# A third up product out of seven small ones, and a down product with a shorter list of waits, in a Strassen mixture-of-experts kernel

## The chip, the cores and the metric

The kernel runs on one core of a Trainium2 chip. The core has five engines that run side by side, each with its own instruction queue: TensorE (PE, matrix products; PEld is its loading of the stationary operand), VectorE (DVE), ScalarE (ACT), GpSimd (POOL) and SyncE (SP, which here only issues transfers). The metric is the device time of one execution in microseconds: the median of the runs shown.

## The reference

Linear attention makes a matrix x of 4608 tokens by 512; a mixture of 8 experts follows, in which every expert sees every token and the routing only weights the sum.

```
P = exp(x @ w_gate - max)              # 4608 x 8, then 8 rounds of scaling rows and columns
out = 0
for e in range(8):
    h   = maximum(x @ w1[e], 0)        # up:   4608x512 @ 512x1024
    out += P[:, e:e+1] * (h @ w2[e])   # down: 4608x1024 @ 1024x512
```

Nearly all the arithmetic is in the up and down products of the eight experts.

## The kernel before

**Stages.** The first 200 us are the attention, with parts of expert 0's products laid between its steps. Then come the routing and the rest of expert 0 in plain products, then experts 1 to 7.

**Seven products for eight.** Experts 1 to 7 use a Strassen form: a 2 by 2 block product is made of seven block products instead of eight, with sums of blocks taken before and after. Tokens stand in nine groups of 512; the first eight are worked in four pairs, the ninth by itself. Within a pair the hidden features are split in two halves (`fp` 0 and 1). One pair and one half make a *unit*; an expert has eight units of pairs and one unit of the ninth group. A unit holds the seven up products of its own pair and half, and the seven down products of a group whose up work was done earlier.

**An up product, plain.** `wide` (line 1467) gives for each of two feature blocks `q` two matmuls with 512 moving columns: four matmuls of 512 for a product. Line 1471 records these.

**An up product, fine.** In experts 2 to 7 two of the seven (the weights "12" with the tokens "21", and "s1" with "t1") are themselves made of seven: `fine` (line 1588 on) gives seven matmuls of 256 columns (line 1603) in four steps a1 to a4, and the sums between them: in a1 two ACT copies of 128x256, one into the side buffer `m5` (1615) and one within PSUM (1617); in a2 a DVE addition (1624); in a3 an ACT copy (1608); and at the end one addition of `m5` (`last`, on DVE at 1644, or `later`, on POOL at 1638). The next step's matmul needs the copy before it, so between a1, a2, a3 and a4 other matmuls have to fill PE. A dictionary `INNER` names the fine products. The product "11", whose steps are called x, is plain: x10 and x11 are its two halves in the written order, and `keep` copies its banks to the buffers k1 on ACT (1666). The order names the steps of fine products wa to wd and ya to yd, with wk and yk for what follows.

**Operands.** In expert 1 the sums of token blocks are made once on DVE (`sub`, line 1239) and sent to DRAM (`Xd` and `Xp` plain, `Xi` for fine products, seven blocks instead of four). In experts 2 to 7 `load_fine` (1385) brings each pair's operands back on the SP queue (1393) into places in the space of `xT`, taken in turn: four places for fine operands (`FINE_X`), two of them used by a pair, and six for plain ones (`PLAIN_X`), five used by a pair. A load waits until the last reader of its place is done. The sums of weight blocks are taken for every expert on DVE, four short additions for each fine product (`fine_up`, 1270 on).

**Down.** `down7` multiplies quarters of h and sums of quarters `S` with blocks of w2, in seven products X1, Y1, Z1, X2, X3, Z2, X4 of eight 256-column matmuls each (1462). X1 reads only the quarter h(0,0). The results leave PSUM on DVE (1855), or on ACT (1867) with the addition on POOL (1870).

**What sets the order.** Every operation is given to a planner with an engine, an estimated duration, and the buffers and keys it reads and writes; the planner lays them on the engines in order of start, ties going to the one written earlier. The written order within a unit is a string of step names, one of 19 in `UNITS`: 0 to 8 for expert 1, 9 to 16 for the eight pair units of experts 2 to 7, 17 for the ninth group, and 18 for the ninth group of the last expert, where it goes first. Each engine then executes its instructions in the planned order. PSUM has eight banks that all products share. DVE operations on two SBUF operands are marked as sharing a port with POOL; the planner keeps the two apart, and a POOL operation planned close behind such a DVE operation is given a wait for it.

Of the kernel before, what the change touches and what calls it, by code (L numbers as in the profile page):

```python
# [349 lines left out]
def kernel(  # L350
# [137 lines left out]
        R[f"H{slot}"].make = lambda i, slot=slot: late["hs"][:, slot]  # L488
    ring("s_p", [128, 1024], BF16, "T", 4)
    ring("s_p", [128, 2, 256], FP32, "U", 4)  # L490
    ring("s_p", [128, 2, 2, 256], BF16, "X", 4)
    ring("s_p", [128, 2, 256], FP32, "K", 4)
    R["K"].make = lambda i: R["X"].make(i).rearrange("p a k c -> p (a k c)").bitcast(
# [843 lines left out]
    class Turns:  # L1337
# [4 lines left out]
        def next(self):  # L1342
# [3 lines left out]
            return p[0], p[1], first  # L1346

    pairs = [(g, g + 1) for g in range(0, 8, 2)]
    INNER = {"12": "21", "s1": "t1"}
    FINE_W = {n: space(3, 1024 * (i + 4 - len(INNER)), 1024, "nfc", (4, 2, 128)) for i, n in enumerate(INNER)}  # L1350
    FINE_X = Turns([space(i // 2, 1792 * (i % 2), 1792, "nc", (7, 256)) for i in range(4)])
    PLAIN_X = Turns([space(2 + i // 4, 1024 * (i % 4), 1024, "akc", (2, 2, 256))
                     for i in range(5 if len(INNER) > 2 else 6)])
    M5 = Turns([space(i, 3584, 512, "c", (256,), FP32) for i in range(2)])

    Xi = {(g[0], n): dram.tile([128, 7, 256], BF16, name=f"xi{g[0]}{n}")
          for g in pairs for n in INNER.values()}
    Xp = {(g[0], n): dram.tile([128, 2, 2, 256], BF16, name=f"xp{g[0]}{n}") for g in pairs
# [212 lines left out]
    def up49(A, fp, X, H, gs, r0):  # L1571
# [16 lines left out]
        def fine(bank, an, xn, more=(), takes=(), wk=(), out_c=None):  # L1588

            f, r = A[an]  # L1590
            s, rs = A[an + "*"]
            t, rt = X[xn]
            r = r + rs + rt + list(r0)
            m5, key, first = M5.next()

            def a(q, k):
                return lambda: f()[:, k, 128 * (2 * fp + q):][:, 0:128]

            def sf(n):
                return lambda: s()[:, n, fp, :]  # L1600

            def mul(q, n, lhs, rhs, more=(), takes=(), start=False, wk=()):
                pe(256, lambda: nc.tensor.matmul(  # L1603
                    halves_of(bank[q], n)(), lhsT=lhs(), rhs=t()[:, rhs, :], start=start,
                    stop=True, skip_group_check=True), r + list(more), [bank[q], *wk], takes)

            def copy(q, n, q2, n2):
                act(293, lambda: nc.scalar.copy(
                    out=halves_of(bank[q], n)(), in_=halves_of(bank[q2], n2)()),
                    [bank[q2]], [bank[q]])  # L1610

            def a1():
                mul(1, 0, sf(0), 3, more, takes, True, wk)
                mul(1, 1, a(0, 0), 0)
                act(256, lambda: nc.scalar.copy(out=m5(), in_=halves_of(bank[1], 0)()),
                    [bank[1]], [key, *first])
                act(293, lambda: nc.scalar.copy(
                    out=halves_of(bank[0], 0)(), in_=halves_of(bank[1], 1)()),
                    [bank[1]], [bank[0]])

            def a2():
                mul(1, 1, sf(1), 4)
                mul(0, 0, a(0, 1), 1)
                dve(256, lambda: nc.vector.tensor_tensor(  # L1624
                    out=halves_of(bank[0], 1)(), in0=halves_of(bank[1], 1)(), in1=m5(),
                    op=ALU.add), [bank[1], key], [bank[0]])

            def a3():
                mul(1, 1, sf(2), 5)
                mul(0, 1, sf(3), 2)  # L1630
                if out_c is None:
                    copy(1, 0, 1, 1)

            def a4():
                mul(1, 0, a(1, 1), 6, start=out_c is not None)

            def later(to, w):
                pool(330, lambda: nc.gpsimd.tensor_tensor(  # L1638
                    out=to(), in0=to(), in1=m5(), op=ALU.add), [key], [w])

            def last(out_=None, w=None, pm=False):
                if pm:
                    return later(out_, w)
                dve(256, lambda: nc.vector.tensor_tensor(
                    out=out_() if out_ else halves_of(bank[1], 1)(),
                    in0=halves_of(bank[1], 1)(), in1=m5(), op=ALU.add),
                    [bank[1], key] if out_ else [key], [w] if out_ else [bank[1]])

            return a1, a2, a3, a4, last
# [63 lines left out]
                        [y[q]])  # L1713

        def yk():
            ys[4](lambda: k1[1]()[:, 1, :], (k1[1], 1), True)
            for q in range(2):
                add(y, q, k1, 1, 1)

        def wk():  # L1720
            keep(w, 0, u)
            act(256, lambda: nc.scalar.copy(out=u[1]()[:, 0, :], in_=halves_of(w[1], 0)()),
                [w[1]], [(u[1], 0)])
            ws[4](lambda: u[1]()[:, 1, :], (u[1], 1))

        def x2(q):
            prod(x, q, "s2", "t2")
# [58 lines left out]
    def down7(e, g, H, B7):  # L1786
# [94 lines left out]
        x, y, z = new("P1"), new("PO"), new("P1")  # L1881

        def X1():
            prod(x, a(0, 0), "11", hk(0, 0), True, sk(1) + hk(1, 0),
                 [("D", e, g)])
            act(512, lambda: nc.scalar.copy(out=y(), in_=x()), [x], [y])

# [31 lines left out]

    END = "X1 p2 Y1 X2 Z1 p3 X3 Z2 X4 p0 p1".split()  # L1920
    UNITS = [o.split() for o in (
# [27 lines left out]
    turns = [int(i) for i in (  # L1949
        "0 1 2 3 4 5 6 7 8 9 10 11 12 13 14 15 16 17 9 10 11 12 13 14 15 16 17 9 10 11 12 "  # L1950
        "13 14 15 16 17 9 10 11 12 13 14 15 16 17 9 10 11 12 13 14 15 16 17 18 9 10 11 12 "
# [102 lines left out]
```

## Time and profile before

| | |
|---|---|
| median of 3 runs (lowest, highest) | 1012.7 us (1012.62, 1013.81) |
| the profiled execution | 1013.51 us, of which the span from first to last instruction is 1011.7 us |
| granted TensorE clock | 1.000 |
| PE matmuls | 8232 |
| DVE, ACT, POOL instructions | 1911, 1786, 466 |
| periods of experts 4, 5 and 6 | 108.1, 107.9 and 108.2 us, from the recurring long piece in the chain (548.95, 657.08, 764.98, 873.22) |

The busy share of an engine is the union of its instructions' spans. A matmul's span is longer than the distance to the next, since matmuls overlap: 273 ns against 109 ns for 256 columns. So the work of PE is read from the chain of work, where a piece of n matmuls in a row has its length beside it, and not from the mean of one. What one engine waited for another is a view of its own.

### The profile page before, as it was taken

Reading aid. Unit: us, or ns where it says so; the run is one execution under the profiler, and the core shown is the slowest. Engines: PE = TensorE matmul, PEld = TensorE weight load, DVE = VectorE, ACT = ScalarE, POOL = GpSimd, SP = SyncE. Lnnn points to the kernel's source line nnn. Section 1 sums busy time; section 2 is a strip of 40 time slices with the busy share of each in tenths; the row PEclk is TensorE's granted clock in tenths of the full one; section 3 lists DMA queues with packets and bytes.
Section 4 is the critical chain, followed back from the end, with each engine's and each line's share of the span. In section 5 each row is a group of like instructions: output and inputs, shape, how many; then the busy total and the mean of one; then the engine's idle time right before and its main releaser. Section 6 shows DMA issues by size and latency. Waiting matters only on the chain.

```text
span 1011.7 us, 22631 instructions
## 1 busy us (share of the span) xinstructions
PE 997.0 (99%) x8232; PEld 712.1 (70%) x8232; DVE 879.9 (87%) x1911; ACT 771.8 (76%) x1786; POOL 412.9 (41%) x466
## 2 busy tenths in 40 slices
PE   7899999999999999999999999999999999999998
PEld 4666666644666877777777777787778777787776
DVE  7999998987888988889888889889888988889885
ACT  7999999845987777767777777777776777677773
POOL 5778674400133333343333334433343343433333
PEclk9999999999999999999999999999999999999999
DMA  9999979181135522273237232452228222724553
GB/s 237 200 200 177 169 141 140 38 172 48 58 103 114 164 89 90 66 173 106 82 96 146 82 113 88 94 146 89 90 75 203 89 90 66 139 90 135 173 180 125
DMA packets 129680, 123.32 MB, mean 122 GB/s; under 512 B 55712, under 2 KB 98720, under 8 KB 129568
## 3 DMA queue, kind: packets, MB, share of 16 engines
q1 hardware_dynamic: 97616, 97.82, 34.5%
q0 software_dynamic: 31648, 23.86, 16.3%
q8 instruction: 64, 1.05, 0.4%
q14 instruction: 48, 0.39, 0.1%
q10 hardware_dynamic: 304, 0.20, 0.1%
HBM read 117.78 MB, written 18.74 MB: 135 GB/s over the span
## 4 chain that ended last, share of the span: by engine, by line
PE 94%; DMA 2%; ACT 2%; DVE 1%; issue 0%; SPq 0%; DVEq 0%
PE ps L1462 42%; PE ps L1471 25%; PE ps L621 18%; PE ps L1603 7%; PE ps L904 2%; DMA acc<-in_q_dram 1%; DMA xT<-wx 1%; ACT q L617 1%; ACT k L617 1%; DVE wx L613 0%; PE ps L751 0%; ACT wx L617 0%; PE ps L933 0%; DVE m L613 0%; DVE ps L912 0%
## 5 line engine op out<-in xcount | busy, mean ns | idle before, releaser
L1870 POOL TENSOR_TENSOR acc<-acc,hx 128x512 f32<-128x512 f32 x186 | 235.1, 1269 | 429.4 <-ACT hx L1867 125.9
L1462 PEld LDWEIGHTS <-hs 128*128 128x128 bf16 x1984 | 193.8, 98 | 54.1 <-issue 0.2
L1867 ACT ACTIVATE hx<-ps,P 128x256 f32<-128x256 f32 x372 | 157.5, 478 | 63.0 <-PE ps L1462 52.6
L1855 DVE SCALAR_TENSOR_TENSOR acc<-ps,P,acc 128x256 f32<-128x256 f32 x372 | 162.6, 478 | 46.7 <-PE ps L1462 33.8
L1471 PE MATMUL ps<-xT,T 128*128 128x512 bf16 x608 | 179.1, 379 | 0.0
L1462 PEld LDWEIGHTS <-hx 128*128 128x128 bf16 x1488 | 145.4, 98 | 32.8
L1462 PE MATMUL ps<-hx,hs 128*128 128x256 bf16 x992 | 134.8, 273 | 0.1
L1670 DVE CUSTOM_DVE_ANT_0 hs<-ps,U 128x512 bf16<-128x512 f32 x192 | 126.9, 682 | 5.7 <-PE ps L1471 5.1
L1676 ACT ACTIVATE hs<-ps 128x512 bf16<-128x512 f32 x96 | 57.5, 599 | 56.5 <-PE ps L1471 56.0
L1471 PEld LDWEIGHTS <-T 128*128 128x128 bf16 x672 | 65.6, 98 | 36.0
L1603 PE MATMUL ps<-xT 128*128 128x256 bf16 x384 | 88.0, 273 | 0.2 <-DVE ps L1624 0.2
L1471 PE MATMUL ps<-xT,wx 128*128 128x512 bf16 x288 | 84.1, 379 | 0.0
L1462 PE MATMUL ps<-wx,hs 128*128 128x256 bf16 x560 | 76.9, 273 | 0.0
L621 PE MATMUL ps<-w,hx 128*128 128x512 bf16 x288 | 73.1, 379 | 0.0
L621 PE MATMUL ps<-xT,w 128*128 128x512 bf16 x288 | 72.9, 379 | 0.0
L1638 POOL TENSOR_TENSOR X<-X,xT 128x256 f32<-128x256 f32 x48 | 34.9, 726 | 91.2 <-DVE hx L1239 34.3
L1728 ACT COPY ps<-ps 128x512 f32<-128x512 f32 x96 | 55.1, 581 | 17.0 <-DVE acc L1855 12.3
L1670 DVE CUSTOM_DVE_ANT_0 hs<-ps,X 128x512 bf16<-128x512 f32 x96 | 65.5, 682 | 2.6 <-PE ps L1603 2.3
L1462 PE MATMUL ps<-wx,hx 128*128 128x256 bf16 x496 | 67.4, 273 | 0.0
L1666 ACT COPY X<-ps 128x512 f32<-128x512 f32 x96 | 57.1, 602 | 13.4 <-PE ps L1471 13.4
L1462 PE MATMUL ps<-hx 128*128 128x256 bf16 x496 | 66.8, 273 | 0.0
L613 DVE TENSOR_REDUCE m<-ps 128x4 f32<-128x512 f32 x88 | 58.7, 679 | 3.7 <-PE ps L621 1.9
(172 smaller groups left out, 2132.0 us busy)
## 6 DMA issues: line engine op xcount, KB each, us to landing
xT<-xd SPq DMA_DIRECT2D x72, 256.0 KB, 2.8
xT<-xp SPq DMA_DIRECT2D x48, 256.0 KB, 2.9
xT<-xi SPq DMA_DIRECT2D x24, 448.0 KB, 3.7
wx<-in_moe_w_dram POOLq DMA_DIRECT2D x8, 1024.0 KB, 12.8
v_m<-in_v_dram SPq DMA_DIRECT2D x15, 512.0 KB, 5.9
out_dram<-acc SPq DMA_DIRECT2D x14, 512.0 KB, 2.9
w<-in_moe_w_dram POOLq DMA_DIRECT2D x6, 1024.0 KB, 11.5
qk<-in_k_dram POOLq DMA_DIRECT2D x12, 256.0 KB, 5.7
```

What stands on the lines that cost most here:

```text
L613: dve(el, lambda: nc.vector.tensor_reduce(out=dst(), in_=src(), axis=AX.X, op=ALU.max, apply_absolute_value=True), r, w)
L621: nc.tensor.matmul(out_, lhsT=lhsT, rhs=rhs, start=start, stop=stop)
L1462: pe(256, lambda i=i, k=k, z=z: nc.tensor.matmul(bank()[:, 256 * i:256 * i + 256], lhsT=lhs(k, i), rhs=rhs(k), start=first and z, stop=k = ...
L1471: pe(512, lambda k=k: nc.tensor.matmul(bank().rearrange("p (a b) -> p a b", a=2), lhsT=lhs(k), rhs=rhs(k), start=first and k == 0, stop=k ...
L1603: pe(256, lambda: nc.tensor.matmul(halves_of(bank[q], n)(), lhsT=lhs(), rhs=t()[:, rhs, :], start=start, stop=True, skip_group_check=True) ...
L1666: act(512, lambda: nc.scalar.copy(out=flat(to[q])(), in_=bank[q]()), [bank[q]], [(to[q], 0), (to[q], 1)])
L1670: dve(515, lambda: nc.vector._custom_dve(ADD_SAT, out=out_(q, i, j), in0=bank[q]().rearrange("p (a b) -> p a b", a=2), in1=to[q](), s0=3.0 ...
L1676: act(512, lambda: nc.scalar.activation(out=out_(q, i, j), in_=bank[q]().rearrange("p (a b) -> p a b", a=2), func=ACT.Relu, bias=0.0, scal ...
L1728: act(512, lambda: nc.scalar.copy(out=z[q](), in_=x[q]()), [x[q]], [z[q]])
L1855: dve(320, lambda n=n, ts=ts: nc.vector.scalar_tensor_tensor(out=acc[g][:, ts, 256 * j:256 * j + 256], in0=bank()[:, 256 * n:256 * n + 256 ...
L1867: act(370, lambda n=n: nc.scalar.activation(out=u()[:, n, :], in_=bank()[:, 256 * n:256 * n + 256], func=ACT.Copy, bias=0.0, scale=P[:, 4 ...
L1870: pool(695, lambda: nc.gpsimd.tensor_tensor(out=acc[g][:, 2 * i:2 * i + 2, 256 * j:256 * j + 256], in0=acc[g][:, 2 * i:2 * i + 2, 256 * j: ...
```

## The change

The product "11" joins the fine ones, in experts 2 to 7: x10 and x11 become xa, xb, xc, xd and xk. With three fine products the fine weights take a third place, the plain token operands five places instead of six (a pair now uses four), and the four fine places now serve three operands of a pair. `m5` gets a third place, in a buffer of its own. After the product "s1" (wk) the addition of `m5` goes from DVE to POOL, and the half copy on ACT before it becomes a whole one. In experts 2 to 7 X1 no longer waits for h(1,0) and for the sum S1. All 19 written orders are new.

```
-    INNER = {"12": "21", "s1": "t1"}
+    INNER = {"11": "11", "12": "21", "s1": "t1"}
...
+    ring("s_p", [128, 256], FP32, "M", 1)
+    m5 = new("M")
+    m5.slot = 0
+    M5.places.append((m5, "M", []))
...
-            def later(to, w):
-                pool(330, lambda: nc.gpsimd.tensor_tensor(
-                    out=to(), in0=to(), in1=m5(), op=ALU.add), [key], [w])
-
-            def last(out_=None, w=None, pm=False):
+            def later(to):
+                for b in to:
+                    pool(330, lambda b=b: nc.gpsimd.tensor_tensor(
+                        out=b()[:, 1, :], in0=b()[:, 1, :], in1=m5(), op=ALU.add),
+                        [key], [(b, 1)])
+
+            def last(out_=None, w=None, pm=()):
                 if pm:
-                    return later(out_, w)
+                    return later(pm)
...
         def yk():
-            ys[4](lambda: k1[1]()[:, 1, :], (k1[1], 1), True)
+            ys[4](pm=k1[1:])
...
         def wk():
             keep(w, 0, u)
-            act(256, lambda: nc.scalar.copy(out=u[1]()[:, 0, :], in_=halves_of(w[1], 0)()),
-                [w[1]], [(u[1], 0)])
-            ws[4](lambda: u[1]()[:, 1, :], (u[1], 1))
+            keep(w, 1, u)
+            ws[4](pm=u[1:])
...
         def X1():
-            prod(x, a(0, 0), "11", hk(0, 0), True, sk(1) + hk(1, 0),
+            prod(x, a(0, 0), "11", hk(0, 0), True, [] if e > 1 else sk(1) + hk(1, 0),
                  [("D", e, g)])
```

The steps of x that the change now calls are in the kernel already, behind the test `"11" in INNER`:

```
        if "11" in INNER:
            xs = fine(x, "11", "11", [], own)
...
        def xk():
            xs[4]()
            for q in range(2):
                if "12" in INNER:
                    keep(x, q, k1)
```

The new orders of the eight pair units (9 to 16):

```
+        "xa xb wa X1 Z1 ya X2 wb xc Y1 X3 xd yb X4 wc yc xk Z2 yd wd wk x20 yk x21 x30 x40 "
+        "w21 x31 x41 w20",
+        "xa Z1 xb wa X1 wb Z2 xc xd wc ya xk x21 X2 wd yb wk yc x20 x30 Y1 x40 X3 yd x31 "
+        "w21 yk w20 X4 x41",
+        "X1 wa wb xa Z1 xb wc ya Y1 X2 wd xc yb xd xk yc Z2 wk x20 X3 yd x21 w21 w20 x30 yk "
+        "x31 X4 x40 x41",
+        "xa X1 Z1 Y1 xb wa ya wb xc X2 yb xd wc xk x20 wd wk x21 yc x31 X3 Z2 x30 x41 x40 "
+        "yd yk w20 w21 X4",
+        "wa wb X1 xa Y1 Z1 xb wc ya yb xc wd xd yc X2 X3 yd xk x21 wk X4 x20 w21 x30 yk x31 "
+        "Z2 w20 x40 x41",
+        "X1 xa xb wa ya yb yc wb wc xc xd xk yd Z1 X2 wd wk x21 Z2 x20 yk X3 X4 x31 x30 Y1 "
+        "x41 w21 x40 w20",
+        "wa xa xb xc X1 wb xd Z1 xk wc X2 Y1 x21 wd ya x20 Z2 wk X3 w21 w20 x30 x31 yb X4 "
+        "yc x41 yd x40 yk",
+        "xa X1 Z1 xb X2 xc xd xk wa Z2 ya yb yc X3 wb x20 x21 yd X4 wc wd yk wk x30 Y1 x40 "
+        "x31 w20 x41 w21",
```

38 rows, old and new, of the table UNITS are left out of this document.

## The prediction

> **What bounds the kernel now.** I read the page's busy times first, then the chain of work, then what PE waited for, then a table by stage.
>
> ```profile
> PE 997.0 (99%) x8232; PEld 712.1 (70%) x8232; DVE 879.9 (87%) x1911; ACT 771.8 (76%) x1786; POOL 412.9 (41%) x466
> PE 94%; DMA 2%; ACT 2%; DVE 1%; issue 0%; SPq 0%; DVEq 0%
> ```
>
> PE is busy 99% of the span and makes 94% of the chain. A busy PE need not be PE at its pace, so the chain is read in order of time, for the distance between matmuls:
>
> ```profile
> 657.08 13.54 PE ps L1462 x124
> 764.98 13.54 PE ps L1462 x124
> 995.08 1.73 PE ps L621 x8
> ```
>
> 124 matmuls of 256 columns in a row take 13.54 us, 109.2 ns each; eight of 512 columns take 1.73 us, 216.3 ns each. With these two prices an expert can be counted. A pair unit has five plain up products of four 512s (20 x 216.3 = 4.33 us), two fine ones of seven 256s (14 x 109.2 = 1.53 us) and a down of 56 x 109.2 = 6.12 us: 11.97 us. Eight of them, and 112 x 109.2 = 12.23 us for the ninth group, are 108.0 us. The two long pieces above lie 107.9 us apart. So in experts 2 to 7 PE has matmuls without a gap, and what PE executes is the time. What PE waited for, from 260 us to 1005 us, is one line:
>
> ```profile
> PE ps L1603 <- DVE ps L1624: 0.2, 1, 0.2
> ```
>
> How much room the others have is in the table by stage (us, then PE, PEld, DVE, ACT, POOL busy, clock, DMA share). The first four rows are experts 3 to 6, 108 us each; the fifth is the start of expert 1; the last two are attention:
>
> ```profile
> 441.00:549.00 108.00, 108.00 (x835) 81.36 (x833) 95.22 (x199) 79.08 (x187) 41.53 (x38) 1.00 0.40 107
> 549.00:657.00 108.00, 107.94 (x833) 81.14 (x831) 95.01 (x199) 78.84 (x185) 41.33 (x38) 1.00 0.40 107
> 657.00:765.00 108.00, 108.00 (x835) 81.36 (x834) 95.23 (x199) 79.01 (x186) 41.57 (x38) 1.00 0.39 107
> 765.00:873.00 108.00, 107.82 (x832) 81.10 (x831) 94.79 (x199) 78.86 (x185) 41.19 (x38) 1.00 0.39 107
> ...
> 258.00:335.00 77.00, 77.00 (x525) 51.10 (x524) 66.17 (x157) 65.29 (x133) 23.08 (x19) 1.00 0.41 107
> ...
> 20.00:60.00 40.00, 36.49 (x454) 25.65 (x454) 39.07 (x91) 39.84 (x101) 31.00 (x53) 1.00 1.26 203
> 60.00:203.00 143.00, 142.82 (x1695) 93.95 (x1692) 131.06 (x308) 135.42 (x330) 91.40 (x147) 1.00 0.89 140
> ```
>
> DVE is at 88% in the experts and ACT at 73%, and PE loses nothing by it. The attention rows show where that ends: from 60 to 203 us, with DVE at 91.7% and ACT at 94.7%, PE lacks 0.18 us of 143; from 20 to 60 us, with DVE at 97.7% and ACT at 99.6%, it lacks 3.51 of 40, 8.8%. The prices of what is added are in the groups by shape:
>
> ```profile
> L1624 DVE TENSOR_TENSOR ps<-ps,xT 128x256 f32<-128x256 f32 x96 | 40.5, 427 | 13.8 <-PE ps L1603 10.1 <-ACT ps L1886 1.4 <-PE ps L1462 1.0
> L1617 ACT COPY ps<-ps 128x256 f32<-128x256 f32 x96 | 36.9, 385 | 0.4
> L1615 ACT COPY xT<-ps 128x256 f32<-128x256 f32 x96 | 36.8, 383 | 8.7 <-PE ps L1603 8.5
> L1608 ACT COPY ps<-ps 128x256 f32<-128x256 f32 x96 | 36.6, 382 | 8.3 <-PE ps L1603 7.7
> L1638 POOL TENSOR_TENSOR X<-X,xT 128x256 f32<-128x256 f32 x48 | 34.9, 726 | 91.2 <-DVE hx L1239 34.3 <-ACT xT L1615 28.3 <-ACT U L1666 19.7
> L1644 DVE TENSOR_TENSOR U<-ps,xT 128x256 f32<-128x256 f32 x48 | 20.1, 419 | 11.9 <-PE ps L1603 11.1
> ```
>
> The counts give the number of units: 96 for two fine products, 48 units.
>
> **The change, part by part.** *The matmuls.* In each of 48 units four 512s (865.2 ns) give way to seven 256s (764.4 ns): 100.8 ns less, 4.84 us in all, and all of it on the path that sets the end, since PE is that path. PE will have 8232 + 48 x 3 = 8376 matmuls.
>
> Three more weight loads a unit come with it, 98 ns each in the groups of PEld. They go beside the matmul before: the 124 matmuls above each had a load of their own and still kept 109.2 ns. The page "TensorE: Matmul & The Clock Gate" of the Trainium skill (section "Back-to-back issue gap") puts it otherwise: in a stream of loads and matmuls it gives about 81 ns a matmul at 128 columns and about 131 at 512. An estimate half-way down its line, 97.7 ns at 256, would make seven small ones 684 ns against 524 for four large ones, a loss of 160 ns a unit or 7.7 us in all. This trace disagrees, 109.2 and 216.3 ns, and the sum goes by the trace.
>
> *DVE.* A unit gains the addition in a2 (427 ns) and the one at the end of x (same form as 1644, taken at 419), and loses the one after w (419): +0.43 us. Each expert gains four short weight sums of 280 ns (the 128x256 bf16 form of line 1239), 1.1 us. An expert goes from 95.1 to 95.1 + 8 x 0.43 + 1.1 = 99.6 us, in 107.9 - 0.8 = 107.1: 93%. *ACT* gains 383 + 385 + 382 in the three copies and 605 - 388 = 217 where half a copy becomes whole, 1.37 us a unit; an expert goes from 79.0 to 89.9 us, 84%. *POOL* gains one addition of 0.73 us a unit, 41.4 to 47.2 us, 44%. None of this is on the path as long as PE finds its banks free and its copies made. The cover is the idle time of DVE, 7.5 us in an expert, and the other matmuls between two steps of a fine product; gone, it costs PE what DVE is late.
>
> What such waits cost at 93% this trace does not show, so I bound it. At best it is nothing, as at 88% now; below nothing it can't be, because PE has no wait left to lose. At worst it is the row from 20 to 60 us, 8.8%, for those stretches in which DVE comes to 97% or more. The nearest row is 60 to 203 us, DVE at 91.7% and ACT fuller than here: 0.18/143 = 0.13%. I take it: 0.13% of 6 x 107.1 us is 0.8 us.
>
> *The addition after w, now on POOL.* Its readers are the DVE additions of x31 and w2. Queued behind it on POOL are the down additions of line 1870 (1.27 us each); these free the buffers of line 1867 on ACT, which waited for POOL only 3.5 us in five times over the whole run. POOL is idle 56% of the time, so I cost it at nothing; if POOL were late, DVE would stand in its queue before x31, and that is the second rival's place.
>
> *X1 without its waits.* PE waits for nothing there now, so nothing is gained; the freedom is in the new order. X1's bank is then taken earlier, a matter of the banks that I put to the 0.8 us. *Expert 1.* A pair's "11" goes to DRAM as seven blocks: 16 DVE sums of 280 ns (4.5 us), four more transfers on SP in all, and four times a buffer of the ring X, for about 3 us each (four sums and a landing of 2.0 us). In the row from 258 us DVE would rise from 66.2 to at most 70.7 of 77 us, 92%, and PE has no wait there: by the same 0.13% 0.1 us, within the rounding. *Loads.* A fine operand has 448 KB against 256, 192 KB more for each of 24 pairs; the DMA engines are at 40%. The load is covered as long as its place comes free in time: that is the first rival. *The new orders* take away nothing, since PE has no gap to close; what they may add is the waits bounded above.
>
> Sum: -4.84 + 0.8 = -4.0 us. The profiled execution took 1013.51 us (its span of 1011.7 and 1.8 around it) and would take 1009.5; it stands 0.8 above the median of the runs, 1012.7, which becomes 1008.7.
>
> **Rivals.** *A late fine operand takes it back.* Until now a pair's two fine operands had two places that the pair before did not use. Now three share four places: "t1" goes where "11" of the pair before lay and "21" where its "t1" was, so the loads wait for xd and wd in the unit before. Counted in the written orders at the two matmul prices, PE has 8.9, 6.7 and 8.9 us of other work between xd and the next wa at the three changes of pair within an expert, and 9.0 to 12.4 us between wd and ya. The fine operands land in 3.7 to 7.6 us (medians of the four groups); the longest landing of an operand between 441 and 873 us was 9.4, when weights stream beside it. So mostly there is time. If one load per expert took 7.6 us against 6.7, PE would lose 0.9 x 6 = 5.4 us, and the time would be 1013.3: no gain. Smaller lateness ends between that and the forecast.
>
> *DVE becomes the bound: slower.* The busiest 12 us of expert 4 shows DVE at 11.45:
>
> ```profile
> 585.00:597.00 12.00, 12.00 (x94) 8.97 (x92) 11.45 (x25) 9.15 (x22) 4.24 (x5) 1.00 0.31 101
> ```
>
> Add 0.43 us and shorten the unit to 11.87, and DVE is full. A full DVE costs PE 8.8% by the row from 20 to 60 us, 1.04 us a unit. One such unit per expert costs 6.3 us in all (1014.1), two 12.5 us (1020.4). It decides from 0.8 us an expert, where the gain is gone. Against it: the work of an expert is laid anew, and the mean of 93% leaves 7.5 us that another order can spread.
>
> The Trainium skill's page "SBUF — State Buffer" (section "SBUF: two separate sides") has a rule that speaks for this rival: a DVE operation with two SBUF inputs and a GpSimd operation hold their port for a whole instruction, and the other blocks. By that rule 48 more POOL operations of 0.73 us could hold DVE up by at most 5.8 us an expert, which would fill it to 98%. In this trace the DVE sums of 512 have a median of 417 to 426 ns with POOL at 41%, so the order keeps them apart so far.
>
> *Weight loads pace the small matmuls.* If a load no longer went beside a matmul, seven times 98 + 109 ns is 1.45 us against 0.87, +28 us in all: 1040.5. The 124 matmuls at 109.2 ns speak against it.
>
> *The step doesn't come about.* Were the planned order to leave "11" plain somewhere, the matmuls would be fewer than 8376 and the time 1012.7; the edit gives no such way.
>
> **How the numbers follow.** From 0.2%, 2.0 us, on a difference can be told. The forecast has 0.65 (1007.4 to 1010: no waits at all gives 1012.7 - 4.8 = 1007.9, and runs differ by some 0.5). The late operand has 0.14, of which 0.05 stays faster and 0.09 ends within 0.2%. DVE as the bound has 0.18, the weight loads 0.02, the step that doesn't come about 0.01. Faster 0.70, same 0.10, slower 0.20. The range goes from 1007.4 to 1014.2: it takes in the forecast, the late operand and one full unit per expert, and leaves out two full units and the weight loads, with less than 0.2.
>
> **What would show it.** Right: 8376 matmuls, 1008 of them at line 1603's place and 992 at 1471's; DVE 1911 + 48 + 16 + 24 = 1999 and ACT 1786 + 144 = 1930 instructions; the recurring long piece about 107.1 us apart; DVE at about 93% and ACT 84% in an expert; waits of PE for DVE and ACT after 260 us of about a microsecond in all. Wrong: PE waiting for a transfer into xT at the start of a pair (first rival); PE waiting for DVE additions in the fine steps, or for banks that DVE frees, with DVE near 97% (second); chain pieces with more than 110 ns a small matmul (third).

## The result, and the profile after

The changed kernel takes 1010.4 us, the median of 8 runs (1008.93 to 1012.13), against 1012.61 for the kernel before on the same chip (8 runs, 1011.9 to 1014.79): a ratio of 0.9976, with a 95% interval of 0.9965 to 0.9986, or -2.2 us. Run once more on another chip, it took 1010.15 against 1012.78. The profiled execution took 1010.62 (span 1008.8), 2.9 less than the one of before, which stood 0.9 above its own median.

Lines have moved by one to six: the down matmul is at 1466 now, the plain up matmul at 1475, the fine one at 1607, the sum of 512 at 1240, the addition of a2 at 1628, the POOL addition at 1643. The busy times of the changed kernel, from its page:

```profile
PE 991.1 (98%) x8339; PEld 726.9 (72%) x8376; DVE 899.2 (89%) x1999; ACT 810.2 (80%) x1930; POOL 446.8 (44%) x514
```

8376 weight loads, 1999 DVE and 1930 ACT instructions are the counts that were forecast: "11" is fine in all 48 units. (37 records of the 8376 matmuls are missing in this trace, all of them of 512 columns, at line 622.) The chain of work breaks off where those records are missing, so its shares say little; read in order of time (start, duration, engine, tile, line, count) it still shows the experts:

```profile
444.13 11.35 PE ps L1466 x104
551.26 11.35 PE ps L1466 x104
658.39 11.35 PE ps L1466 x104
765.52 11.35 PE ps L1466 x104
...
997.00 1.73 PE ps L622 x8
```

The piece comes back every 107.13 us, where the kernel before needed 107.9 to 108.2, and 11.35/104 is 109.1 ns a small matmul. The table by stage of the changed kernel (us, then PE, PEld, DVE, ACT, POOL busy, clock, DMA share) has experts 3 and 4 and then the start of expert 1:

```profile
441.00:548.00 107.00, 107.00 (x857) 83.65 (x856) 97.17 (x210) 85.23 (x210) 46.98 (x45) 1.00 0.41 115
548.00:655.00 107.00, 107.00 (x857) 83.71 (x856) 97.16 (x211) 85.25 (x210) 46.95 (x45) 1.00 0.40 115
...
258.00:335.00 77.00, 75.74 (x514) 50.03 (x513) 70.07 (x174) 64.66 (x132) 22.32 (x18) 1.00 0.47 126
```

DVE has gone from 88% to 90.8%, ACT from 73% to 79.7%, and PE is still busy for 107.00 of 107.00 us. The third row is new: PE lacks 1.26 us of 77, where it lacked nothing before. What PE waited for from 260 to 1005 us is again one line, now at that place:

```profile
PE ps L1475 <- DVE hs L1530: 1.3, 2, 0.7
```

So the fine experts gave what was forecast, and part of it is given back in expert 1, which has no fine product on PE at all. To see how much, I set the distance between the starts of matmuls against their pace: 109.2 ns for each one of 256 columns and 215.8 ns for each one of 512, missing records filled in from the weight loads. (The 40 matmuls of 8 and 24 columns in the routing are taken at their own distances, 25 and 28 ns.) What is over is called *lost time* below. PE's work by this count is 976.98 us before and 972.22 after, -4.76. This figure is the number of matmuls times their pace, the sum of the forecast again; that the pace was kept is what the period of 107.13 us shows. Lost time from 203 us on is 0.7 us before; it is 3.1 in the profile of the changed kernel and 2.1 in that of its second run. By stage:

| lost time, us | before | after | second run of after |
|---|---|---|---|
| 203 to 320 (expert 0's rest, expert 1) | 0.09 | 0.47 | 0.26 |
| 320 to 335 (expert 1, last pair) | 0.01 | 1.58 | 0.83 |
| 350 to 441 (turn to expert 2, and expert 2) | 0.01 | 0.26 | 0.26 |
| 441 to 873 (four experts) | 0.60 | 0.12 | 0.12 |
| 873 to the last matmul | 0.00 | 0.67 | 0.67 |

From the start of the last matmul to the end of the span it takes 4.25 us where it took 3.87; what makes the difference wasn't followed. -4.76 + 1.4 to 2.4 + 0.4 is -2.0 to -3.0, where the medians lie. The rest between the two profiles, 0.9 us, lies before 203 us, in the attention, which the change doesn't touch.

**Where the 1.3 us arise.** The transfers between 300 and 335 us, first of the kernel before, then of the changed one (size, median us from issue to landing):

```profile
w<-in_moe_w_dram POOLq DMA_DIRECT2D x2, 1024.0 KB, 11.5
...
xi6t<-X SPq DMA_DIRECT2D x1, 256.0 KB, 2.0
```

```profile
w<-in_moe_w_dram POOLq DMA_DIRECT2D x2, 1024.0 KB, 11.9
...
xi6t<-X SPq DMA_DIRECT2D x1, 256.0 KB, 8.0
```

This store of the last fine operand takes 8.0 us to land where it took 2.0. The issue of expert 2's weights on POOL, before and after, points at the cause:

```profile
319.78 1.69 POOL L516 DMA_DIRECT2D w<-in_moe_w_dram  x2
```

```profile
314.54 1.69 POOL L517 DMA_DIRECT2D w<-in_moe_w_dram  x2
```

Before, the weights were issued 1.9 us behind the store (317.93), and the store was all but alone. The new orders let them start 5.2 us earlier, 1.8 us ahead of the store (316.38), which then lands beside 2 MB of weights, at 324.4. It holds a buffer of the ring X, and DVE and then PE stand behind that (timelines of the changed kernel, DVE and PE; idle time before the instruction and its releaser in brackets):

```profile
324.41 0.42 DVE L1240 TENSOR_TENSOR X<-xT 128x512 bf16<-128x512 bf16 x1 [1.70 <-DMA xi6t<-X]
```

```profile
329.63 0.38 PE L1475 MATMUL ps<-X,wx 128*128 128x512 bf16 x1 [0.54 <-DVE hs L1530]
330.72 0.81 PE L1475 MATMUL ps<-X,wx 128*128 128x512 bf16 x3 [0.71 <-DVE hs L1530]
```

DVE stands for 1.70 us, and its evictions behind that come 0.54 and 0.71 us late for PE.

### The profile page after: what moved, and what is told of

The parts are those of the page before. It is cut to its first block, busy times and chain, and to the rows that moved or that the text cites. A ratio compares the mean times of both kernels' runs of the same rounds, so it can differ in the third digit from the quotient of the medians.

```text
span 1008.8 us, 23319 instructions
## 1 busy us (share of the span) xinstructions
PE 991.1 (98%) x8339; PEld 726.9 (72%) x8376; DVE 899.2 (89%) x1999; ACT 810.2 (80%) x1930; POOL 446.8 (44%) x514
## 4 chain that ended last, share of the span: by engine, by line
PE 66%; DVE 1%; issue 0%
PE ps L1466 39%; PE ps L1475 16%; PE ps L1607 11%; PE ps L622 1%; DVE hs L1676 0%; DVE hs L1530 0%; DVE acc L1860 0%; DVE X L1240 0%; DVE acc L1774 0%; DVE ps L1628 0%
## 5 line engine op out<-in xcount | busy, mean ns | idle before, releaser
L1475 PE MATMUL ps<-xT,T 128*128 128x512 bf16 x608 | 167.4, 379 | 0.0
L1676 DVE CUSTOM_DVE_ANT_0 hs<-ps,U 128x512 bf16<-128x512 f32 x192 | 123.7, 683 | 4.4 <-PE ps L1475 1.4
L1607 PE MATMUL ps<-xT 128*128 128x256 bf16 x576 | 127.4, 272 | 0.1
L1466 PE MATMUL ps<-wx,hx 128*128 128x256 bf16 x496 | 73.7, 273 | 0.0
L1466 PE MATMUL ps<-hx 128*128 128x256 bf16 x496 | 72.8, 273 | 0.0
L622 PE MATMUL ps<-w,hx 128*128 128x512 bf16 x274 | 69.9, 379 | 0.6
L1607 PEld LDWEIGHTS <-xT 128*128 128x128 bf16 x576 | 56.3, 98 | 16.6 <-issue 0.2
L1466 PE MATMUL ps<-w,hx 128*128 128x256 bf16 x432 | 63.0, 273 | 0.0
L1612 ACT COPY ps<-ps 128x256 f32<-128x256 f32 x144 | 53.0, 376 | 9.9 <-PE ps L1607 9.9
L1466 PE MATMUL ps<-w,hs 128*128 128x256 bf16 x432 | 60.9, 273 | 0.0
```

The source lines that it names most:

```text
L622: nc.tensor.matmul(out_, lhsT=lhsT, rhs=rhs, start=start, stop=stop)
L1466: pe(256, lambda i=i, k=k, z=z: nc.tensor.matmul(bank()[:, 256 * i:256 * i + 256], lhsT=lhs(k, i), rhs=rhs(k), start=first and z, stop=k = ...
L1475: pe(512, lambda k=k: nc.tensor.matmul(bank().rearrange("p (a b) -> p a b", a=2), lhsT=lhs(k), rhs=rhs(k), start=first and k == 0, stop=k ...
L1607: pe(256, lambda: nc.tensor.matmul(halves_of(bank[q], n)(), lhsT=lhs(), rhs=t()[:, rhs, :], start=start, stop=True, skip_group_check=True) ...
L1612: act(293, lambda: nc.scalar.copy(out=halves_of(bank[q], n)(), in_=halves_of(bank[q2], n2)()), [bank[q2]], [bank[q]])
L1676: dve(515, lambda: nc.vector._custom_dve(ADD_SAT, out=out_(q, i, j), in0=bank[q]().rearrange("p (a b) -> p a b", a=2), in1=to[q](), s0=3.0 ...
```

## The experiments

Two theories stood against each other at first. **A**: the loss is that held buffer in expert 1, and the load of DVE costs nothing. **B**: DVE, fuller by the fine "11", takes the gain back. Beside them I took the change apart: X1's waits, the fineness of "11", the POOL addition, the four places of fine operands. Each ratio is to the kernel before, run on the same chip (medians 1012.78, 1012.78 and 1012.99 in the three groups); with each comes its distance to the changed kernel, taken at 1010.15.

**The changed kernel again.**

> The changed kernel again, as the yardstick of this group. Theory A (the product saves 4.8 us of PE work; about 1.6 us of new waits are given back, 1.25 of them in expert 1 at one place): 2 to 3 us faster than before, DVE near 97.2 us of 107 in an expert, the same two waits of PE for the addition of expert 1 at 329 to 331 us. Theory B (the rest of the forecast was lost to DVE being full): the same time, but waits of PE for DVE in every expert.

Measured: 1010.15 us, ratio 0.9971 (0.996 to 0.9983). The same loss is in its profile, in the same place, but smaller: the store takes 7.3 us to land, and PE waits 0.7 us, once, for line 1530.

**Was it the fineness of "11"?** In `eleven_plain_again` "11" is plain as before, and all else of the change stays (X1 without waits, the additions on POOL, the new orders with the fine steps taken out of them). Here and below a diff is against the changed kernel where nothing else is said.

```
-    INNER = {"11": "11", "12": "21", "s1": "t1"}
+    INNER = {"12": "21", "s1": "t1"}
...
-        "xa Z1 xb wa X1 wb Z2 xc xd wc ya xk x21 X2 wd yb wk yc x20 x30 Y1 x40 X3 yd x31 "
-        "w21 yk w20 X4 x41",
+        "x10 Z1 wa X1 wb Z2 x11 wc ya x21 X2 wd yb wk yc x20 x30 Y1 x40 X3 yd x31 "
+        "w21 yk w20 X4 x41",
```

> The changed kernel with product eleven plain as before (INNER of two; in the new orders xa stands for x10, xc for x11, and xb, xd and xk fall out); X1 freed, the addition after w on POOL, the new orders stay. PE's work is that of before, 4.8 us more than the changed kernel. Theory A (the gain is the work of the product, the rest gives nothing): 1012.5 to 1014 us, at or above before. Rival (freed X1, POOL and new orders bring part of the gain): under 1012 us.

Measured: 1013.52 us, ratio 1.0009 (1.0 to 1.0018), 3.4 above the changed kernel. PE's counted work is back at 976.98. So the rest of the change gives nothing by itself (in orders made for three fine products), and the fine "11" is worth 3.1 to 3.4 us net of the waits that it brings.

**X1 freed alone, and X1 bound again.** `x1_freed_alone` is the kernel before, its old orders kept, with only X1's waits shortened (diff against the kernel before); `x1_waits_again` is the changed kernel with X1's waits as they were. These waits are entries in the planner's list: X1 reads only h(0,0), so what they change is the order in which the operations are laid.

```
-            prod(x, a(0, 0), "11", hk(0, 0), True, sk(1) + hk(1, 0),
+            prod(x, a(0, 0), "11", hk(0, 0), True, [] if e > 1 else sk(1) + hk(1, 0),
```

```
-            prod(x, a(0, 0), "11", hk(0, 0), True, [] if e > 1 else sk(1) + hk(1, 0),
+            prod(x, a(0, 0), "11", hk(0, 0), True, sk(1) + hk(1, 0),
```

> The kernel before, with nothing but X1 freed of its waits for h(1,0) and S1 in experts 2 to 7; old orders, eleven plain. As the prediction had it: nothing to gain, within 0.5 us of before. Rival (the freedom is worth something by itself): PE's few waits, 0.6 us after 260 us, can't give more than 0.6 us; a loss would come from banks taken earlier.

> The changed kernel, with X1 waiting for h(1,0) and S1 again; the written orders stay. Theory A (PE has other matmuls there): within 0.7 us of the changed kernel. Rival (the three fine products need X1 early to fill PE between their steps): waits of PE at the beginning of units, 0.1 us or more a unit, 5 us or more in all.

Measured: freed alone 1016.16 us, ratio 1.0033 (1.002 to 1.0046), slower by 3.4; bound again 1060.72 us, ratio 1.0467 (1.0453 to 1.0481), 50.6 above the changed kernel. That was the largest effect of all, and the prediction had nothing of the kind: in `x1_waits_again` PE loses 8.2 to 8.5 us in each of experts 2 to 6 and 9.7 in the last. The two longest of its waits there, from 203 us on:

```profile
PE ps L1607 <- ACT ps L1621: 10.2, 31, 0.6
PE ps L1607 <- DVE ps L1628: 8.3, 18, 0.7
```

Both are in the fine steps, behind the copies and additions between them. DVE is busy for less of its time there than in the changed kernel (91.58 of 107 us against 97.17), and ACT as well (80.92 against 85.23): the engines are not full, PE only has to sit through their chain. One such place in expert 3, PE's timeline of `x1_waits_again`:

```profile
487.24 0.27 PE L1607 MATMUL ps<-xT 128*128 128x256 bf16 x1
...
487.78 0.27 PE L1607 MATMUL ps<-xT,wx 128*128 128x256 bf16 x1
488.62 0.27 PE L1607 MATMUL ps<-xT 128*128 128x256 bf16 x1 [0.57 <-ACT ps L1621]
488.73 0.27 PE L1607 MATMUL ps<-xT,wx 128*128 128x256 bf16 x1
489.19 0.27 PE L1607 MATMUL ps<-xT 128*128 128x256 bf16 x1 [0.19 <-ACT ps L1621]
...
490.42 0.38 PE L1607 MATMUL ps<-xT 128*128 128x256 bf16 x2 [0.69 <-DVE ps L1628]
```

Six fine matmuls stand in a row, 0.65 us of work, and then each next step has to wait for a copy or an addition. A down product with its short list of waits is what fills these gaps in the changed kernel. With the old orders, which don't need it, the same freedom costs 3.4 us. PE's lost time from 203 us on is 2.7 us there against 0.7, and from 441 to 873 us waits of 1.5 us out of 1.7 end with line 1624's additions: a shorter list of waits alone moves the planned order, and not for the better.

**The addition after w back on DVE, then both.** First `w_addition_on_dve`, then `both_additions_on_dve`, which has this and `yk`'s addition on DVE as well. They put load on DVE and take it off POOL; for w, ACT's copy is halved again too.

```
-            keep(w, 1, u)
-            ws[4](pm=u[1:])
+            act(256, lambda: nc.scalar.copy(out=u[1]()[:, 0, :], in_=halves_of(w[1], 0)()),
+                [w[1]], [(u[1], 0)])
+            ws[4](lambda: u[1]()[:, 1, :], (u[1], 1))
```

```
-            ys[4](pm=k1[1:])
+            ys[4]()
```

> The changed kernel, with the addition after w on DVE again and the half copy before it. DVE gets 8 x 0.42 = 3.4 us more in an expert, ACT 1.7 and POOL 5.8 less. Theory A (DVE has room up to about 95%): within 1 us of the changed kernel. Theory B (DVE near its limit; between 0.13% of waits at 91.7% and 8.8% at 97.7% a straight line gives about 3% at 94%): some 10 to 20 us slower than the changed kernel.

> The changed kernel with the additions after w and after y both on DVE (none on POOL). Against the run with w's alone another 0.42 us a unit, 3.4 us an expert, on DVE. If PE's loss grows with DVE's load along the line from the changed kernel (97.2 of 107 us, next to no waits) over w alone (98.8 of 107, 0.6 us an expert): 1 to 1.5 us of waits an expert, 1017 to 1020 us. If the loss in the run with w alone came from the later end of its chain and not from the load: about 1014 us.

Measured: 1013.75 us, ratio 1.0008 (0.9999 to 1.0016), and 1017.51, ratio 1.0047 (1.0034 to 1.006). Moving the one addition to POOL is thus worth 3.6 us, and the second 3.8. For the first, neither theory had the size: A had nothing much, B three times that and more. Expert 3 in the table by stage, of the first and of the second kernel:

```profile
441.00:548.00 107.00, 106.96 (x852) 83.08 (x850) 98.53 (x217) 83.63 (x209) 41.36 (x37) 1.00 0.40 113
```

```profile
441.00:548.00 107.00, 106.88 (x847) 82.55 (x846) 100.56 (x223) 82.38 (x207) 35.74 (x29) 1.00 0.41 113
```

Beside the row of the changed kernel this makes a scale over experts 3 to 6: with DVE at 90.8% PE loses 0.03 us an expert, at 92.1 to 92.5% 0.55 to 0.69, at 94.0 to 94.8% 1.0 to 1.5. Operations of DVE end 1.8 of the 2.5 us that PE waits in these four experts in the first of the two kernels, and 2.7 of 4.5 in the second; ACT ends the rest. So B's mechanism is there, and the changed kernel stands just ahead of it. But the share alone doesn't set the loss: each edit also moves the planned order, and the kernel before lost 0.15 us an expert with DVE at 88%, the one with X1 freed 0.35 to 0.57.

**The weights behind the last store.** In `weights_after_last_store` both of expert 2's weight loads are planned behind the stores of the last pair's fine operands; in `w2_after_last_store` only the second is. As with X1, this binds the planner and puts no wait into the transfer itself.

```
-        w1, w2 = load_w(e, ["late", ("acc", 4, 0, 0)] if e > 1 else ["late"])
+        w1, w2 = load_w(e, (["late", ("acc", 4, 0, 0)] if e > 1 else ["late"])
+                        + [("Xi", 6, n, 2) for n in INNER.values() if e == 2])
```

```
-                r, [(w, i, j) for i in range(2) for j in range(2)])
+                r + ([("Xi", 6, n, 2) for n in INNER.values()] if e == 2 and w is w2 else []),
+                [(w, i, j) for i in range(2) for j in range(2)])
```

> The weight loads of expert 2 wait for the last stores of fine operands. Theory A (the last store of a fine operand lands 8.0 us late because the weights stream beside it; its buffer of ring X is then late for the sums of the ninth group, DVE stands 1.7 us, PE 1.25): that store lands in about 2 us, both waits go, 1.2 us less than the changed kernel unaltered, 3.4 to 4 us less than before. Rival (DVE is simply too full in expert 1 with 16 more sums): the same sums stand there, PE still waits about a microsecond, the time is that of the changed kernel.

> Only the second of expert 2's two weight loads (w2, which the down products need a unit later) waits for the last stores of fine operands; w1 goes as in the changed kernel. Theory A (the late landing is what holds DVE in expert 1, and holding back both loads only moved the loss to the beginning of expert 2, where w1 came late): the last store lands in about 5 us instead of 8, PE's waits at 329 to 331 us go, none comes at the beginning of expert 2, 0.7 to 1.3 us less than the changed kernel, so 3.3 to 3.9 us less than before. Rival (any delay of the weights costs more than it gives): slower than the changed kernel by 1 us or more.

Measured: 1015.69 us, ratio 1.0027 (1.0019 to 1.0036), 5.5 above the changed kernel, and 1011.01, ratio 0.9985 (0.9976 to 0.9994), 0.9 above it by the medians (the interval overlaps that of the changed kernel). The store of the first of these, from its transfers between 300 and 335 us, and then what PE waited for from 260 us on:

```profile
xi6t<-X SPq DMA_DIRECT2D x1, 256.0 KB, 2.0
```

```profile
PE ps L1466 <- ACT hx L1872: 2.0, 2, 1.0
PE ps L1607 <- DVE ps L1628: 1.2, 2, 1.0
```

This shows the cause named above: with the weights issued at 321.36, behind it, the store lands in 2.0 us again, and PE's waits behind line 1530 are gone. (In the other kernel, w1 went off 1.9 us ahead of the store and w2 4.2 us behind it, before it had landed; the store took 7.0 us.) But the time is not saved. PE loses 1.15 us from 334.0 to 335.2, the first of its two waits for line 1872, and 4.3 us from 350 to 441, in expert 2, at the second of them and at fine steps whose filling now lies elsewhere.

**The buffer instead of the weights.** The same wait can go another way: the four temporaries that the store holds are put into the ring T, for the last pair alone (`last_temporary_elsewhere`) or for all (`all_temporaries_elsewhere`). The core of the edit, first of the former, then of the latter:

```
-        y = new("X")
+        last = g == 6
+        y = new("T" if last else "X")
```

```
-        y = new("X")
+        y = new("T")
```

> The changed kernel, but the fine sums of the last pair of expert 1 are made in a spare buffer of the ring T instead of ring X, so that the sums of the ninth group need not wait for their store; the weights go when they went. Theory A (that buffer is what DVE waits for): DVE's wait of 1.7 us for the store goes, and PE's waits at 329 to 331 us go but for the part that DVE's own load makes (0.4 us in the run with only w2 held back): 0.5 to 1.2 us less than the changed kernel, 3 to 3.5 us less than before. Rival (the place is only where DVE's load shows, and the loss moves): no gain against the changed kernel.

> The same for all four pairs of expert 1. Theory A: as the run with the last pair alone, within 0.5 us, unless the sums of the first pair, which then go earlier, among the routing's short DVE steps, hold these up: then up to 1 us more.

Measured: 1017.83 us, ratio 1.005 (1.0037 to 1.0063), and 1015.32, ratio 1.0026 (1.0017 to 1.0035). The weights went off 1.0 and 1.2 us ahead of the store, and it took 7.8 us to land in both, but it no longer holds a buffer of the ring X. Lost time from 320 to 335 us is 0.14 and 0.00, so the wait in expert 1 is gone in both; from 350 to 441 it is 7.3 and 6.4. PE's timeline at the first fine steps of expert 2, first in the changed kernel and then with all temporaries elsewhere:

```profile
354.07 0.38 PE L1466 MATMUL ps<-wx,hx 128*128 128x256 bf16 x2
354.29 0.27 PE L1607 MATMUL ps<-xT,w 128*128 128x256 bf16 x1
354.40 0.27 PE L1466 MATMUL ps<-wx,hx 128*128 128x256 bf16 x1
354.51 0.27 PE L1607 MATMUL ps<-xT 128*128 128x256 bf16 x1
```

```profile
354.03 0.27 PE L1607 MATMUL ps<-xT,w 128*128 128x256 bf16 x1
354.81 0.55 PE L1607 MATMUL ps<-xT 128*128 128x256 bf16 x2 [0.51 <-ACT xT L1619]
356.98 0.71 PE L1607 MATMUL ps<-xT 128*128 128x256 bf16 x4 [1.63 <-DVE ps L1628]
358.19 0.37 PE L1607 MATMUL ps<-xT,w 128*128 128x256 bf16 x1 [0.49 <-ACT ps L1612]
358.70 0.58 PE L1475 MATMUL ps<-xT,T 128*128 128x512 bf16 x1
```

In the changed kernel fine and down matmuls alternate; here the fine ones follow one another, since the down matmuls were already spent, and three waits of 2.6 us together come of it. The clock then adds to them (same kernel, table by stage):

```profile
354.00:356.00 2.00, 0.84 (x5) 0.31 (x4) 1.97 (x6) 1.04 (x3) 0.16 (x1) 1.00 0.00 0
356.00:358.00 2.00, 0.71 (x4) 0.38 (x4) 1.23 (x4) 0.51 (x2) 0.72 (x1) 0.93 0.00 0
358.00:360.00 2.00, 1.67 (x6) 0.72 (x6) 1.02 (x2) 2.00 (x7) 0.22 (x1) 0.50 0.00 0
360.00:362.00 2.00, 2.00 (x8) 0.76 (x7) 0.99 (x2) 1.38 (x3) 0.50 (x1) 0.72 0.00 0
```

The granted clock was 0.50 from 358 to 360 us and 0.72 from 360 to 362, which makes PE lose up to 1.6 us more (2 x 0.50 + 2 x 0.28), nearly all of it after the waits had ended.

**Expert 1 in its old orders.** `old_orders_in_expert_1` gives expert 1 the nine orders of the kernel before, two of them here:

```
-        "x11 y11 x21 x10 x20 w11 Z1 w10 x31 x30 w21 X1 x40 X2 X3 y10 X4 Z2 x41 Y1 w20",
-        "x11 X1 w11 Y1 w10 x10 x21 x20 w20 x31 x30 w21 Z1 X2 X3 Z2 X4 y11 x41 x40 y10",
...
+        "X1 x10 Y1 Z1 y10 w10 x20 x30 x11 Z2 X2 x40 w11 x21 w21 X3 x31 y11 X4 w20 x41",
+        "w10 Z1 x10 x20 x30 X1 X2 w20 x11 X3 Y1 x21 w11 y11 x31 x41 w21 x40 y10 X4 Z2",
...
```

> The changed kernel with the nine written orders of expert 1 as before the change. Theory A (the weights of expert 2 then go later, after the last store, as they did before, when that store landed in 2.0 us): DVE's wait for the store goes; 0.5 to 1.2 us less than the changed kernel, unless DVE, 4.5 us fuller in expert 1, makes PE wait elsewhere. Rival (the new orders of expert 1 are needed because of the 16 more sums): waits of PE for DVE in expert 1, 1 us or more, and slower than the changed kernel.

Measured: 1018.22 us, ratio 1.0054 (1.0041 to 1.0066), 8 us above the changed kernel. The weights are issued at 327.33 here, behind the store, which lands in 2.0 us, and DVE no longer waits for it. PE still loses 1.2 us in expert 1 at another place (0.8 of it at 300 us), and 8.0 us from 350 to 441, again at fine steps without filling (0.85 us on line 1621, 0.59 on 1872, and smaller ones) and by a lower clock behind them (below).

**Three places for the fine operands instead of four.** This is a harder case than the first rival, the late operand, which the changed kernel doesn't show.

```
-    FINE_X = Turns([space(i // 2, 1792 * (i % 2), 1792, "nc", (7, 256)) for i in range(4)])
+    FINE_X = Turns([space(i // 2, 1792 * (i % 2), 1792, "nc", (7, 256)) for i in range(3)])
```

> The changed kernel with three places for fine operands instead of four, so that each of the three is loaded only when the pair before has used its own up to the last step: the first rival of the prediction made true. If late operands cost what the prediction worked out (other work of about a unit between the last use and the next first use is shorter here, since the first product of a unit needs its operand at once): PE waits for transfers into xT at changes of pair, 1 to 5 us in each expert, 1016 to 1040 us. If the planner's order hides it: within 1 us of the changed kernel.

Measured: 1033.38 us, ratio 1.0208 (1.0194 to 1.0222), 23 us above the changed kernel. The three longest waits of PE from 260 us on:

```profile
PE ps L1466 <- ACT ps L1891: 3.2, 6, 0.6
PE ps L1607 <- DMA xT<-xi: 2.5, 1, 2.5
PE ps L1466 <- DVE hx L1240: 2.1, 6, 0.4
```

Only one of these is a transfer, 2.5 us at one place; the rest are again waits for ACT and DVE, 3.3 to 3.5 us of lost time in each of experts 2 to 6 and 9.8 in the last. With four places the trace of the changed kernel has no wait of PE for a transfer from 260 us on.

## Why the prediction was right, and where it was off

*PE's work: right.* -4.84 us were forecast, and the count of the trace gives -4.76. 48 units x 100.8 ns come out of the spacing of matmuls before the change, and the test of it is the period: the long piece was to come back every 107.1 us and does every 107.13. The counts of matmul loads, DVE and ACT instructions were right to the one.

*The waits: the step that was mis-sized.* The prediction put 0.8 us for them, as 0.13% of the six fine experts. The sum was thus -4.0, and -2.2 to -2.6 was measured. The fine experts have next to none: 0.12 us in the four of the middle, less than before. What PE lost instead, 1.4 to 2.4 us more than before, lies in expert 1, at the turn to expert 2 and in the last expert, and 0.4 more behind the start of the last matmul. "Below nothing it can't be, because PE has no wait left to lose" was misread, too: the rows of experts 4 and 6 before show PE lacking 0.06 and 0.18 us, and by the count the four experts gave back 0.48 us of such losses. For expert 1 the prediction had 0.1 us, from DVE's share of the stage. It did name the thing that failed: "four times a buffer of the ring X, for about 3 us each (four sums and a landing of 2.0 us)". The landing was 8.0 us, because the new orders send expert 2's weights off 5.2 us earlier, ahead of that store. I had taken a median landing from a trace in which store and weights happened not to meet, and had read a stage's wait off the busy share of an engine. `weights_after_last_store` shows that the meeting is the cause of the long landing and of the wait. That the whole loss stayed at 1.8 to 2.8 us was luck in part: beyond 0.1 us for expert 1 the sum had no term for the joints between stages, and nothing in the working kept them small.

*What the wait was worth: less than it looked.* These 0.8 to 1.6 us were not to be had by themselves in what was tried. Five edits of expert 1 took the wait away wholly or in part (the weights later, both or one; the temporaries elsewhere, one pair's or all; the old orders), and none came out below the changed kernel: +0.9, +5.2, +5.5, +7.7 and +8.1 us. In the four slow ones PE loses 4.3 to 8.0 us from 350 to 441 us, at the first fine steps of expert 2. That the filling between these steps is gone is seen in the sequence of matmuls; why the planned order in each case spends the down products earlier wasn't traced and stays open. A fifth buffer for the ring X, which might take the wait away and leave the rest, wasn't tried.

*X1: half right.* "PE waits for nothing there now, so nothing is gained; the freedom is in the new order" holds for the old orders (freed alone, X1 even costs 3.4 us). But the step said nothing of what the new orders are without it: 50 us slower. The prediction had the cover in one clause, "the other matmuls between two steps of a fine product", and priced the cover of DVE's idle time only. The rival that was missing is this one: DVE and ACT not full, but PE's filling in the wrong place. The rows shown would have given it a price: a copy of 0.38 us or an addition of 0.43 stands between one step and the next, against 0.11 for a matmul.

*The POOL addition: cost right, gain not stated.* Costing it at nothing held: POOL is at 44%, as forecast (46.98 of 107 us), and the two groups of the addition take 727 and 728 ns, against 726 before. That the move is worth 3.6 us, with PE losing 0.6 us an expert where DVE is at 92%, was not in the prediction, which kept the price of a full DVE (8.8%) as the far end and 0.13% as the near one. The far end was no clean price of DVE either: from 20 to 60 us before, the waits of PE that the trace names end with DVE for 1.6 us, with ACT for 0.8 and with a transfer for 0.4. The losses between the two ends are measured now.

*DVE's and ACT's shares: too high.* 93% and 84% were forecast by adding mean durations, 90.8% and 79.7% measured. Instructions in a row overlap in these records: two evictions of 682 ns each take 1.28 us (`321.43 1.28` in DVE's timeline), and in expert 3 after the change DVE's durations add up to 111.1 us within 97.2 busy ones, ACT's to 103.2 within 85.2. So a sum of durations overstates the busy time.

*The rivals.* The late operand didn't come: four places suffice, three would have cost 23 us, where the rival had 5.4 for a load that comes late; only 2.5 of the 23 are a wait of PE for a transfer. DVE as the bound didn't come, but by little: one addition more a unit takes the whole gain. The weight loads are dead: 109.1 ns from one small matmul to the next, in rows of 104. The page "TensorE: Matmul & The Clock Gate" of the Trainium skill (section "Back-to-back issue gap"), from whose figures the prediction's estimate made seven small matmuls cost 160 ns more than four large ones, is not borne out: the period of an expert, 107.9 to 108.2 us before, is 107.13 now.

## What to carry to other kernels

Where the bound engine runs without gaps, count its work by the distance between its instructions: that put the new period of an expert at 107.1 us, and 107.13 were measured. Price the waits at the joints between stages and not by an engine's mean share: look at which buffers a store holds, and what else will be on the DMA engines when a new order moves that other transfer. And when small dependent products replace a large one, ask first which independent matmuls lie between the steps; a plan that loses them costs far more here (5 to 50 us) than the sums and copies themselves, and a wait removed in one place can bring that about in another.

## What the runs showed of the hardware that was not expected

A 256 KB store on SP's queue landed in 2.0 to 2.4 us in the five profiles here in which the weights went off from POOL's queue 1.9 us or more behind it, and in 7.0 to 8.0 us in the nine in which one load of 1 MB or both had gone off 1.0 to 1.9 us ahead of it.

Short waits were paid twice in two runs in which several came together. With all temporaries elsewhere PE waited 0.51, 1.63 and 0.49 us within 3.9 us (354.3 to 358.2), and the granted clock was 0.93 from 356 to 358 us and 0.50 from 358 to 360, with matmuls of 512 columns 0.43 us apart (from 359.29 to 359.72 a 512, from 359.08 to 359.29 a 256) instead of 0.216. In the old orders of expert 1 the clock was 0.60 from 364 to 368 us, after four waits of 1.9 us together from 358.3 on. With only the last pair's temporaries elsewhere it stayed at 1.00, with six waits of 2.8 us together between 354.5 and 364. The page "TensorE: Matmul & The Clock Gate" of the Trainium skill (section "What's actually happening") knows a half and a full rate, set by PE's activity in windows of about 3.4 us, with the half rate after an idle window. The rate of 0.50 agrees; the window before it wasn't idle, though, since PE was busy for 1.55 of the 4 us from 354 to 358.
